# A spectral mixer beside a shift-MLP on one core: the order of the first stage, and the place of the last layer norm

## The chip, the cores and the metric

One Trainium2 chip, one of its cores. The metric is device microseconds of one execution; a kernel is run several times, and the median is taken. Engines are named as in the profile: PE is TensorE (PEld its weight loads), DVE is VectorE, ACT is ScalarE, POOL is GpSimd, SP is SyncE, which here issues the DMAs.

## The reference

x is 1 x 2048 x 448 in float32 (S = 2048 tokens, D = 448), w1 and w2 are 448 x 448, w3 is 448 x 1792, w4 is 1792 x 448, w_r and w_i are 2048 x 225.

```python
def _A_ref(x, w_r, w_i):                       # spectral branch
    X = rfft2(x, axes=(-2, -1))
    X = X * (w_r + 1j * w_i)
    return irfft2(X, s=(S, D), axes=(-2, -1))

def _B_ref(x, w1, w2, w3, w4):                 # shift-MLP branch
    h = gelu_tanh(layernorm(x) @ w1)           # 2048 x 448
    c = D // 4                                 # 112: four quarters of the columns
    g0 = h[:, :, 0*c:1*c] shifted by +1 token, zeros at the edge
    g1 = h[:, :, 1*c:2*c] shifted by -1
    g2 = h[:, :, 2*c:3*c] shifted by +2
    g3 = h[:, :, 3*c:   ] shifted by -2
    x1 = x + concatenate([g0, g1, g2, g3]) @ w2
    h2 = gelu_tanh(layernorm(x1) @ w3) @ w4
    return x1 + h2

xn = layernorm(A_x)                            # no weights, eps 1e-5
return A_x + _A_ref(xn, A_w_r, A_w_i) + _B_ref(xn, B_w1, B_w2, B_w3, B_w4)
```

## The kernel before

**Tiles.** The tokens lie in 16 blocks of 128 rows, `xb(b)`. The first stage goes over four groups of four blocks, `GRP = [[14,15,0,1],[2,3,4,5],[6,7,8,9],[10,11,12,13]]`, here called group 0 to 3 (in the prediction the first, second and third group are 0, 1 and 2). Each float32 product is made as three float16 products of high and low halves: `PASS = ((0,0),(0,1),(1,0))`, a high half being a cast copy and a low half the rest after subtracting it.

**The first stage, for one group.** `norm1` takes statistics of the four blocks (lines 309 and 310, DVE; `stats1` can take some of them earlier), forms `va` and a first approximation `vy` of the inverse root (lines 333 to 336), the negative mean `nma` (338), and normalises each block in place (line 348 on DVE or POOL, line 345 on ACT, as its list of engines says). It returns two pieces of work that POOL does later: `refine` (lines 356 to 365: small steps that refine the root and end in `gsc`, the scale for the gelu) and `scales` (lines 369 to 376). `turn_pe` transposes the group on PE, 16 transposes of 128 x 128 in four banks (line 396); `turn_copy` makes the high half on ACT (406) and the low half on DVE (407). `w1_in` makes the 44 products with w1 (line 446). `w1_unit` takes one block from there: gelu (465) and high half (466) on ACT, low half on DVE (467), and a transposing DMA on SP's queue (470) that brings the block's h into `hT`.

**The second product.** `w2_tile(b)` makes twelve products (line 486) in the order k = 2, 0, 1, 3 of the quarters, since quarter k reads h of the tokens b - SHIFT[k]; line 488 adds the result to x. Tile 0 needs h of groups 0 and, for its last quarter, block 2, which is the first of group 1; tile 1 needs for its last two quarters blocks 2 and 3. The third of the DMAs of group 1 and later ones are not needed by these two tiles.

**Weights.** `squares` and `powers` find a power-of-two scale of each weight matrix: ACT sums squares, PE adds over partitions (line 254, a product with one column), DVE makes the exponent. `split_w` then makes high and low halves, on engines chosen by its arguments: for w1 the first half on DVE, then ACT with DVE (lines 284, 285) or, for t = 2 and 3, POOL's scaling (279), ACT's copy (281) and POOL's subtraction (282); for w2 quarters 2 and 0 wholly on POOL (274 to 276), quarters 1 and 3 on POOL, ACT and POOL.

**Later stages.** `ln2` is the second layer norm of four blocks: it centres x (line 511 on the engine of its list, 509 for ACT), and makes the two halves (519 on ACT, 520 and 522 on DVE) and a transposing DMA (524). `front` (products with w3, line 417; gelu 731, halves 733 and 734) and `back` (products with w4, line 753) are the channel MLP over eight pairs of blocks G and seven pieces fp. `do_fold`, `step1_in` and `step1` (lines 543 to 579) prepare and make the first transform of the spectral branch: ACT normalises, POOL folds (554 to 557), ACT and DVE make the halves xh (564, 565), PE multiplies (574). These stand between pieces of the MLP, for G = 0 to 2. `w_scale` reads the spectral weights' largest value through a stage buffer of side 1.

**What sets the order.** A scheduler orders each engine's instructions by its own model of time. `behind(key)` restricts it: what is written inside is issued after the instructions noted in `after[key]`. It is an order of issue and not a wait at run time. The lists `PACE`, `FOLD`, `WMAX` and `LATE` give, for the folds, the spectral weights and the last `ln2`, the piece (G, fp) of the MLP behind which a step is issued. Engines work their queues in order. PSUM banks are taken by tags ("mm", "tr", "acc", "sp"), two of each.

**Ahead of all** stand matmuls on a constant, `warm_up` and `warm_rows` (lines 789 and 794), which compute nothing.

Of the kernel before, what the change touches and what calls it, by code (L numbers as in the profile page):

```python
# [36 lines left out]
LATE = [(0, 6), (0, 6), (1, 2), (1, 2)]  # L37
# [84 lines left out]
def body(tc, nc, x, wf, w1, w2, w3, w4, c_g, c_n, c_small, out):  # L122
# [145 lines left out]
    def split_w(hi, lo, src, s, low=None, high=None):  # L268
# [4 lines left out]
        if high is P:  # L273
            P.tensor_scalar(out=src, in0=src, scalar1=s, scalar2=0.0, op0=ALU.mult, op1=ALU.add)
            P.tensor_scalar(out=hi, in0=src, scalar1=1.0, scalar2=0.0, op0=ALU.mult, op1=ALU.add)
            i = P.tensor_tensor(out=lo, in0=src, in1=hi, op=ALU.subtract)
            return (i.ins,)
# [46 lines left out]
    def norm1(g, apply, seen=0, mid=None):  # L324
# [13 lines left out]
        i = V.scalar_tensor_tensor(out=nm, in0=mv[:, :n, 0], scalar=-1.0, in1=y[:, n:], op0=ALU.mult, op1=ALU.mult)  # L338
        if mid:
            mid()  # L340
# [14 lines left out]
        def refine():  # L355
# [9 lines left out]
            P.tensor_scalar(out=gsc[:, 4 * g:4 * g + 4], in0=r[:, n:], scalar1=r1, scalar2=None, op0=ALU.mult)  # L365
# [13 lines left out]
        return refine, scales  # L379
# [60 lines left out]
    def w1_in(g, units, ts, passes=range(3)):  # L440
        for p in passes:
            for t in ts:
                for i, pm in units:
                    wi, xi = ((0, 0), (0, 4), (4, 0))[p]
                    if t < 3 or p != 1:
                        T.matmul(pm[:, :D], xTs[g][:, xi + t, 128 * i:128 * i + 128], w1p[:, wi + t],  # L446
                                 start=t == 0 and p == 0, stop=t == 3 and p == 2)
# [9 lines left out]
    def w1_unit(g, i, pm=None):  # L457
# [7 lines left out]
        A.activation(out=pm, in_=pm, func=AF.Gelu_apprx_tanh, scale=gsc[:, c:c + 1])  # L465
# [8 lines left out]
    def w2_tile(b):  # L474
        pm = bank("sp", f"pw2_{b}")
        n = 0
        for k in (2, 0, 1, 3):
# [7 lines left out]
            for hi, wi in ((0, 0), (0, 1), (1, 0)):  # L485
                T.matmul(pm[:, :D], hT[g][:112, 4 * hi + k, o:o + 128], w2p[:, wi, k], start=n == 0, stop=n == 11)  # L486
                n += 1
        V.scalar_tensor_tensor(out=xb(b), in0=xb(b), scalar=cs[:, CS[b]:CS[b] + 1], in1=pm[:, :D],
                               op0=ALU.mult, op1=ALU.add)

    def ln2(bs, engines, pins=None):
# [8 lines left out]
        for m in range(0, n, 2):  # L500
            w = stage(f"y{b0 + m}", 8 * 448, (b0 + m) // 2 % 2, F16)
# [289 lines left out]
    def warm_rows(n):  # L791
        for i in range(n):
            for h, to in ((0, wps), (64, wps2)):
                T.matmul(to, wsrc[h:h + 64, 0:128], wsrc[h:h + 64], start=True, stop=True)

    wps2 = bank("mm", "wps2")
    warm_up(12)
    warm_rows(1)
    warm_up(2)
    warm_rows(2)  # L800
    warm_up(WARM - 21)
# [35 lines left out]
    with behind("p1"):  # L837
        pts = [turn_pe(0, t) for t in range(4)]
# [3 lines left out]
    for t in range(4):  # L842
        with behind("w1", t - 1):
            turn_copy(0, t, pts[t])
        with behind("a0", t):
            after["w1", t] = split_w(w1p[:, t], w1p[:, 4 + t], w1s[:, t], s1, P if t > 1 else V) if t else (hi, low())
    h1 = pc.tile([128, 1], F32, name="h1")
    V.tensor_scalar(out=h1, in0=s1, scalar1=2.0 ** -5, scalar2=None, op0=ALU.mult)
    for t in range(4):
        w1_in(0, list(enumerate(first)), [t])  # L850
    with behind("ws"):
        n1[0][0]()
    with behind("w1", 1):
# [3 lines left out]
    with behind("n", 1):  # L857
        s2, r2 = powers(m2, 1, "2", first[0][:, 448:512], lambda: stats1(2, [0]))
    with behind("np", 1):
        n1[1][0]()  # L860
        for k in (2, 0):
            after["w2p"] = split_w(w2p[:, 0, k], w2p[:, 1, k], w2s[:112, k], s2[:112], high=P)
    with behind("p2"):
        T1(1)
# [4 lines left out]
    p12, eps12 = s12[:, 1:2], s12[:, 2:3]  # L869
    with behind("a1"):  # L870
        w1_unit(0, 0, first[0])
        n1.append(norm1(2, [P, V, A, P], 1))
    with behind("a1"), behind("n", 2):
        for k in range(1, 4):
            w1_unit(0, k, first[k])
    with behind("na", 2):
        for k in (1, 3):
            split_w(w2p[:, 0, k], w2p[:, 1, k], w2s[:112, k], s2[:112], P)
# [6 lines left out]
    n1[2][0]()  # L885
    with behind("np", 2):
        n1[0][1]()
    for n in n1[1:]:
        n[1]()
# [3 lines left out]
    for k in range(4):  # L893
        w1_unit(2, k)
# [6 lines left out]
    for b in range(4):  # L901
# [130 lines left out]
```

## Time and profile before

| | us |
|---|---|
| median of 3 runs | 416.75 |
| lowest, highest | 415.66, 417.54 |
| the profiled execution | 416.13 |
| its span (all instructions) | 414.3 |
| PE busy | 407.0 |
| DVE busy | 301.2 |
| ACT busy | 245.8 |
| POOL busy | 115.9 |

The profile is of one execution; its span begins with the first and ends with the last instruction, and 1.8 us of the execution lie outside it. The times in rows are from the span's start. A row of the timeline has the start, the busy time, the engine, the line, the operation with the names of what it writes and reads, the shapes and how many instructions are put together (xN); a bracket tells the idle time of the engine before it and what ended it. "x2mem" and "hs" are both buffers of h before its transposing DMA. The mean granted PE clock of the execution was 0.999 of full speed.

### The profile page before, as it was taken

The numbers are of one execution on the slowest core, as the hardware profiler recorded it, in microseconds if no ns is written. First come the engines' busy times: TensorE is split into PE (matmuls) and PEld (weight loads), VectorE is DVE, ScalarE is ACT, GpSimd is POOL, SyncE is SP. The second block draws the span as 40 slices with busy tenths as digits, with TensorE's granted clock in tenths as the row PEclk, the third lists the DMA queues.
The fourth block names the chain that finished last, engine by engine and source line by source line (L and its number), as shares of the span: only waits on it lengthen the run. The fifth ranks groups of instructions, "written<-read, shape, count | busy, mean of one in ns | idle before, by whom it ended". The sixth has DMA issues, their size and how long they took to land.

```text
span 414.3 us, 8527 instructions
## 1 busy us (share of the span) xinstructions
PE 407.0 (98%) x3309; PEld 289.4 (70%) x3309; DVE 301.2 (73%) x636; ACT 245.8 (59%) x425; POOL 115.9 (28%) x206
## 2 busy tenths in 40 slices
PE   8999999999999999999999999999999999999996
PEld 3655555765667677776888788787777776677885
DVE  5998999798775867752688889865777687667122
ACT  4588969964649765642578888864444334342321
POOL 2797720101046647400032121210212221221000
PEclk9999999999999999999999999999999999999999
DMA  8959798804931565215056665620000213224001
GB/s 282 349 184 189 148 170 319 162 37 94 219 91 45 134 221 181 91 46 140 14 129 168 152 162 142 147 70 10 2 0 2 68 31 126 90 67 134 24 0 46
DMA packets 53496, 48.53 MB, mean 117 GB/s; under 512 B 37600, under 2 KB 48480, under 8 KB 53456
## 3 DMA queue, kind: packets, MB, share of 16 engines
q1 hardware_dynamic: 53456, 47.99, 43.0%
q8 instruction: 26, 0.43, 0.4%
q14 instruction: 14, 0.11, 0.1%
HBM read 35.52 MB, written 3.67 MB: 95 GB/s over the span
## 4 chain that ended last, share of the span: by engine, by line
PE 88%; DVE 6%; ACT 2%; DMA 2%; issue 1%; POOL 0%
PE pw L417 31%; PE acc L753 30%; PE pw L486 9%; PE pw L446 4%; PE pu L676 3%; PE ps L574 2%; PE pe L696 2%; PE pp L631 2%; PE px L648 2%; PE py L718 2%; DVE sta L309 1%; DMA xt<-x 1%; DMA h<-hs 1%; DVE xT L407 1%; ACT xf L548 1%
## 5 line engine op out<-in xcount | busy, mean ns | idle before, releaser
L417 PE MATMUL pw<-x2mem,w3p 128*128 128x256 f16 x1232 | 149.1, 273 | 0.0
L753 PE MATMUL acc<-w4p,hf 128*128 128x448 f16 (+1 forms) x714 | 138.0, 341 | 0.0
L417 PEld LDWEIGHTS <-w3p 128*128 128x128 f16 x1232 | 118.6, 98 | 18.9
L753 PEld LDWEIGHTS <-hf 128*128 128x128 f16 x714 | 69.4, 98 | 48.5 <-DVE hf L734 0.3
L731 ACT ACTIVATE pw<-pw,pe 128x512 f32<-128x512 f32 x56 | 36.8, 657 | 68.5 <-PE pw L417 68.5
L734 DVE SCALAR_TENSOR_TENSOR hf<-pw,h,hf 128x512 f16<-128x512 f32 x56 | 41.9, 748 | 42.9 <-ACT hf L733 42.5
L486 PE MATMUL pw<-w2p,h 112*128 112x448 f16 x192 | 39.8, 352 | 0.9 <-DMA h<-hs 0.9
L733 ACT ACTIVATE hf<-pw,h 128x512 f16<-128x512 f32 x56 | 38.2, 684 | 1.2
L657 POOL TENSOR_TENSOR z<-te 128x450 f32<-128x450 f32 x16 | 16.3, 1018 | 74.0 <-DVE te L655 74.0
L446 PE MATMUL pw<-w1p,xT 128*128 128x448 f16 x176 | 35.0, 352 | 0.1
L703 POOL TENSOR_TENSOR e<-e 128x226 f32<-128x226 f32 x16 | 11.3, 708 | 77.6 <-ACT e L700 74.7
L486 PEld LDWEIGHTS <-h 112*128 112x128 f16 x192 | 18.6, 98 | 17.0 <-DMA h<-hs 1.1
L446 PEld LDWEIGHTS <-xT 128*128 128x128 f16 x176 | 17.1, 98 | 16.2 <-DVE xT L407 0.4
L638 ACT ACTIVATE pf<-pp 64x450 f16<-64x450 f32 x32 | 17.3, 541 | 16.6 <-DVE pf L639 8.1
L700 ACT ACTIVATE e<-pe 128x452 f32<-128x452 f32 x16 | 8.8, 548 | 26.6 <-PE pe L696 26.5
L639 DVE TENSOR_TENSOR pf<-pp,pf 64x450 f16<-64x450 f32 x32 | 19.9, 622 | 5.3 <-ACT pf L638 5.0
L653 ACT ACTIVATE te<-px 64x450 f32<-64x450 f32 x32 | 17.2, 539 | 0.5
L557 POOL TENSOR_TENSOR f<-xr 128x452 f32<-128x452 f32 x16 | 16.9, 1078 | 0.6
L711 DVE TENSOR_TENSOR vh<-e,vh 128x448 f16<-128x448 f32 x16 | 10.0, 625 | 9.7 <-ACT vh L710 9.7
L554 POOL TENSOR_TENSOR xr<-xf 128x452 f32<-128x452 f32 x8 | 9.1, 1137 | 24.9 <-issue 24.2
L705 DVE TENSOR_TENSOR e<-e 128x113 f32<-128x113 f32 x16 | 9.5, 594 | 7.8 <-POOL e L703 7.8
L565 DVE TENSOR_TENSOR xh<-f,xh 128x452 f16<-128x452 f32 x16 | 12.8, 842 | 2.0 <-ACT xh L564 2.0
(173 smaller groups left out, 604.2 us busy)
## 6 DMA issues: line engine op xcount, KB each, us to landing
wc<-wf SPq DMA_DIRECT2D x32, 225.0 KB, 3.7
wl<-wf SPq DMA_DIRECT2D x8, 450.0 KB, 4.0
xf<-x SPq DMA_DIRECT2D x8, 448.0 KB, 4.1
xt<-x SPq DMA_DIRECT2D x3, 896.0 KB, 12.6
w3raw<-w SPq DMA_DIRECT2D x3, 896.0 KB, 15.7
xr<-x SPq DMA_DIRECT2D x12, 224.0 KB, 2.5
out<-xr SPq DMA_DIRECT2D x12, 224.0 KB, 2.0
gn<-c_g SPq DMA_DIRECT2D x16, 128.0 KB, 3.3
```

Of the source, the lines that this page charges most:

```text
L417: T.matmul(ps_out, wp[:, wi + t, cols], xT[:, xi + t, tok], start=t == 0 and wi + xi == 0, stop=t == 3 and wi == 4)
L446: T.matmul(pm[:, :D], xTs[g][:, xi + t, 128 * i:128 * i + 128], w1p[:, wi + t], start=t == 0 and p == 0, stop=t == 3 and p == 2)
L486: T.matmul(pm[:, :D], hT[g][:112, 4 * hi + k, o:o + 128], w2p[:, wi, k], start=n == 0, stop=n == 11)
L557: P.tensor_tensor(out=f[:, :, k:k + 2].rearrange("p b s d -> p s b d"), in0=u[:, :, 0], in1=u[:, :, 1], op=op)
L638: A.activation(out=hi, in_=src, func=AF.Copy)
L639: V.tensor_tensor(out=lo, in0=src, in1=hi, op=ALU.subtract)
L653: A.activation(out=e[64 * h:64 * h + 64], in_=px_[64 - 64 * h:128 - 64 * h, :2 * DF], func=AF.Copy)
L657: P.tensor_tensor(out=z, in0=t[:, 0], in1=t[:, 1], op=ALU.add)
L731: A.activation(out=pm, in_=pm, func=AF.Gelu_apprx_tanh, scale=r3)
L733: i = A.activation(out=h[:, 0], in_=pm, func=AF.Copy, scale=h3)
L734: j = V.scalar_tensor_tensor(out=h[:, 1], in0=pm, scalar=h3, in1=h[:, 0], op0=ALU.mult, op1=ALU.subtract)
L753: m = T.matmul(to, h[:, hi, o:o + 128], w4p[0][:, wi, f, r], start=f == 0 and n == 0, stop=f == 13 and n == 2)
```

## The change

It does the following.

- The warm-up is 25 full matmuls; before it was 18 full ones and three pairs of matmuls on half the rows, mixed.
- Group 0: two of the four turns are made first, then four products (t = 0, first pass), then the other two turns, then the rest. The low half of w1's second quarter (t = 1) is made by POOL, through a scaled copy in a scratch row, instead of by DVE.
- `refine` ends before `gsc`, which is a piece of its own (`gain`). POOL's `refine` of group 0 runs uncut after w1's low halves, and that of group 1 uncut after `gsc` of group 0; w2's halves come after `gsc` of group 1: first the scaling of quarters 1 and 3, then scaling and high half of 2 and 0, then the low halves.
- Group 1: two of its turns are placed before the last pass of t = 3 of group 0's products, the other two behind. `powers` of w2 has a bank of its own, and its scalar steps on DVE stand between DVE's low copies.
- Group 2: two of its statistics are taken after group 1's copies, and va, vy and nma stand ahead of the low halves of h of blocks 14 and 15. Its normalisations are on POOL once and DVE three times (before POOL, DVE, ACT, POOL); the DVE ones stand behind these two low halves.
- In group 0, each gelu from the third on is issued behind the halves of the block two before it.
- `w2_tile` 0 and 1 are made in full before group 2's products with w1 (`behind("w2", 1)`); before, the scheduler mixed them.
- The last `ln2` (blocks 12 to 15) is issued behind the MLP's pieces (2,2) to (2,5) instead of (0,6) and (1,2), in the program after the folds, with ACT centring all four blocks, and both its buffers on side 0 of the stage.

```diff
@@ -34,7 +34,7 @@
 FOLD = [(0, 5), (1, 0), (1, 1), (1, 3), (1, 4), (1, 6), (2, 0), (2, 2)]
 PIN = [("a3",), ("a3",), ("a3",), ("a3",)]
 WMAX = [(1, 4), (1, 5), (1, 6), (2, 0), (2, 1), (2, 2), (2, 3), (2, 4)]
-LATE = [(0, 6), (0, 6), (1, 2), (1, 2)]
+LATE = [(2, 2), (2, 3), (2, 4), (2, 5)]
 HS = 3
 INV, LAG = 4, 2
 EVAC, FILL = 0, 100000
@@ -272,9 +272,13 @@
             return i.ins, lambda: V.scalar_tensor_tensor(out=lo, in0=src, scalar=s, in1=hi, op0=ALU.mult, op1=ALU.subtract).ins
         if high is P:
             P.tensor_scalar(out=src, in0=src, scalar1=s, scalar2=0.0, op0=ALU.mult, op1=ALU.add)
-            P.tensor_scalar(out=hi, in0=src, scalar1=1.0, scalar2=0.0, op0=ALU.mult, op1=ALU.add)
-            i = P.tensor_tensor(out=lo, in0=src, in1=hi, op=ALU.subtract)
-            return (i.ins,)
+            i = P.tensor_scalar(out=hi, in0=src, scalar1=1.0, scalar2=0.0, op0=ALU.mult, op1=ALU.add)
+            return i.ins, lambda: P.tensor_tensor(out=lo, in0=src, in1=hi, op=ALU.subtract)
+        if isinstance(low, bass.AP):
+            P.tensor_scalar(out=low, in0=src, scalar1=s, scalar2=0.0, op0=ALU.mult, op1=ALU.add)
+            i = A.activation(out=hi, in_=src, func=AF.Copy, scale=s)
+            j = P.tensor_tensor(out=lo, in0=low, in1=hi, op=ALU.subtract)
+            return i.ins, j.ins
         if low is P:
             i = P.tensor_scalar(out=src, in0=src, scalar1=s, scalar2=0.0, op0=ALU.mult, op1=ALU.add)
             after["ws"] = (i.ins,)
@@ -336,8 +340,10 @@
         V.tensor_scalar(out=yi, in0=yi, scalar1=-1, scalar2=0x5F3759DF, op0=ALU.mult, op1=ALU.add)
         nm = pc.tile([128, n], F32, name=f"nma{b0}")
         i = V.scalar_tensor_tensor(out=nm, in0=mv[:, :n, 0], scalar=-1.0, in1=y[:, n:], op0=ALU.mult, op1=ALU.mult)
+        after["c", g] = (i.ins,)
         if mid:
-            mid()
+            with behind("c", g):
+                mid()
         for k, b in enumerate(bs):
             y_, m_ = y[:, n + k:n + k + 1], nm[:, k:k + 1]
             if apply[k] is A:
@@ -362,7 +368,10 @@
             P.tensor_tensor(out=z, in0=z, in1=q, op=ALU.mult)
             P.tensor_scalar(out=z, in0=z, scalar1=-0.5 * 0.375 ** 3, scalar2=1.5 * 0.375, op0=ALU.mult, op1=ALU.add)
             P.tensor_tensor(out=r, in0=z, in1=w, op=ALU.mult)
-            P.tensor_scalar(out=gsc[:, 4 * g:4 * g + 4], in0=r[:, n:], scalar1=r1, scalar2=None, op0=ALU.mult)
+
+        def gain():
+            i = P.tensor_scalar(out=gsc[:, 4 * g:4 * g + 4], in0=r[:, n:], scalar1=r1, scalar2=None, op0=ALU.mult)
+            after["g", g] = (i.ins,)
 
         def scales():
             c, r1st, u = cs[:, 4 * g:4 * g + 4], w[:, 0:n], w[:, n:]
@@ -376,7 +385,7 @@
             P.tensor_scalar(out=nm1, in0=nm1, scalar1=-1.0, scalar2=None, op0=ALU.mult)
             for k, b in enumerate(bs):
                 xn_scale[b], xn_bias[b] = r1st[:, k:k + 1], nm1[:, k:k + 1]
-        return refine, scales
+        return refine, gain, scales
 
     after = {}
 
@@ -443,8 +452,9 @@
                 for i, pm in units:
                     wi, xi = ((0, 0), (0, 4), (4, 0))[p]
                     if t < 3 or p != 1:
-                        T.matmul(pm[:, :D], xTs[g][:, xi + t, 128 * i:128 * i + 128], w1p[:, wi + t],
-                                 start=t == 0 and p == 0, stop=t == 3 and p == 2)
+                        m = T.matmul(pm[:, :D], xTs[g][:, xi + t, 128 * i:128 * i + 128], w1p[:, wi + t],
+                                     start=t == 0 and p == 0, stop=t == 3 and p == 2)
+        return m
 
     hs_buf = [p1.tile([128, 2, 4, 128], F16, name=f"hs{i}") for i in range(HS)]
     for t in hs_buf:
@@ -462,7 +472,8 @@
         pm = pm[:, :D]
         pv_ = pm.rearrange("p (k n) -> p k n", k=4)
         h = hs_buf[c % (HS if g == 3 else HS + 2)]
-        A.activation(out=pm, in_=pm, func=AF.Gelu_apprx_tanh, scale=gsc[:, c:c + 1])
+        with behind(0, i - 2) if g == 0 and i > 1 else contextlib.nullcontext():
+            A.activation(out=pm, in_=pm, func=AF.Gelu_apprx_tanh, scale=gsc[:, c:c + 1])
         u = A.activation(out=h[:, 0, :, 0:112], in_=pv_, func=AF.Copy, scale=h1)
         v = V.scalar_tensor_tensor(out=h[:, 1, :, 0:112], in0=pv_, scalar=h1, in1=h[:, 0, :, 0:112],
                                    op0=ALU.mult, op1=ALU.subtract)
@@ -483,8 +494,9 @@
             g, i = WHERE[src]
             o += h_at(g, i) - 1
             for hi, wi in ((0, 0), (0, 1), (1, 0)):
-                T.matmul(pm[:, :D], hT[g][:112, 4 * hi + k, o:o + 128], w2p[:, wi, k], start=n == 0, stop=n == 11)
+                m = T.matmul(pm[:, :D], hT[g][:112, 4 * hi + k, o:o + 128], w2p[:, wi, k], start=n == 0, stop=n == 11)
                 n += 1
+        after["w2", b] = (m.ins,)
         V.scalar_tensor_tensor(out=xb(b), in0=xb(b), scalar=cs[:, CS[b]:CS[b] + 1], in1=pm[:, :D],
                                op0=ALU.mult, op1=ALU.add)
 
@@ -498,7 +510,7 @@
         nm = pc.tile([128, 4], F32, tag="nm", bufs=2, name=f"nm{b0}")[:, :n]
         P.tensor_scalar(out=nm, in0=mv[:, :n, 0], scalar1=-1.0, scalar2=None, op0=ALU.mult)
         for m in range(0, n, 2):
-            w = stage(f"y{b0 + m}", 8 * 448, (b0 + m) // 2 % 2, F16)
+            w = stage(f"y{b0 + m}", 8 * 448, 0 if pins else (b0 + m) // 2 % 2, F16)
             o.append(w[:, 0:4 * D].bitcast(F32).rearrange("p (i n) -> p i n", i=2))
             y.append(w[:, 4 * D:8 * D].rearrange("p (i n) -> p i n", i=2))
             for i in range(2):
@@ -788,17 +800,7 @@
         for i in range(n):
             T.matmul(wps, wsrc[:, 0:128], wsrc, start=True, stop=True)
 
-    def warm_rows(n):
-        for i in range(n):
-            for h, to in ((0, wps), (64, wps2)):
-                T.matmul(to, wsrc[h:h + 64, 0:128], wsrc[h:h + 64], start=True, stop=True)
-
-    wps2 = bank("mm", "wps2")
-    warm_up(12)
-    warm_rows(1)
-    warm_up(2)
-    warm_rows(2)
-    warm_up(WARM - 21)
+    warm_up(WARM)
     m1, m2, m3, m4 = (pc.tile([128, n], F32, name=f"m{i}") for i, n in ((1, 4), (2, 1), (3, 4), (4, 7)))
     junk4 = row().bitcast(F16)[:, :2 * D]
     V.memset(m1, 0.0)
@@ -835,74 +837,96 @@
     with behind("n", 0):
         s1, r1 = powers(m1, 4, "1", "mm")
     with behind("p1"):
-        pts = [turn_pe(0, t) for t in range(4)]
+        pts = [turn_pe(0, t) for t in range(2)]
     h_alloc(0)
     first = [bank("mm" if k < 2 else "sp", f"pw1_0{k}") for k in range(4)]
     hi, low = split_w(w1p[:, 0], w1p[:, 4], w1s[:, 0], s1, high=V)
     for t in range(4):
+        if t == 1:
+            after["T", 0] = (w1_in(0, list(enumerate(first)), [0], [0]).ins,)
+            pts += [turn_pe(0, 2), turn_pe(0, 3)]
         with behind("w1", t - 1):
             turn_copy(0, t, pts[t])
         with behind("a0", t):
-            after["w1", t] = split_w(w1p[:, t], w1p[:, 4 + t], w1s[:, t], s1, P if t > 1 else V) if t else (hi, low())
+            after["w1", t] = split_w(w1p[:, t], w1p[:, 4 + t], w1s[:, t], s1, P if t > 1 else xr[:, 0:D]) if t else (hi, low())
     h1 = pc.tile([128, 1], F32, name="h1")
     V.tensor_scalar(out=h1, in0=s1, scalar1=2.0 ** -5, scalar2=None, op0=ALU.mult)
-    for t in range(4):
-        w1_in(0, list(enumerate(first)), [t])
+    for t in range(3):
+        w1_in(0, list(enumerate(first)), [t], range(0 if t else 1, 3))
+    after["T", 1] = (w1_in(0, list(enumerate(first)), [3], [0]).ins,)
     with behind("ws"):
         n1[0][0]()
-    with behind("w1", 1):
+    with behind("a0", 1):
         n1.append(norm1(1, [P, V, A, V]))
     with behind("w1", 3):
         squares(m2[:112], flat(w2s[:112]))
     with behind("n", 1):
-        s2, r2 = powers(m2, 1, "2", first[0][:, 448:512], lambda: stats1(2, [0]))
+        pts = [turn_pe(1, t) for t in range(2)]
+        with behind("T", 1):
+            s2, r2 = powers(m2, 1, "2", "acc", lambda: stats1(2, [0]))
+        with behind("p2"):
+            after["T", 1] = (w1_in(0, list(enumerate(first)), [3], [2]).ins,)
     with behind("np", 1):
+        n1[0][1]()
+    with behind("g", 0):
         n1[1][0]()
-        for k in (2, 0):
-            after["w2p"] = split_w(w2p[:, 0, k], w2p[:, 1, k], w2s[:112, k], s2[:112], high=P)
-    with behind("p2"):
-        T1(1)
+        n1[1][1]()
+    pts += [turn_pe(1, 2), turn_pe(1, 3)]
+    for t in range(4):
+        turn_copy(1, t, pts[t])
+    with behind("g", 1):
+        for k in (1, 3):
+            P.tensor_scalar(out=w2s[:112, k], in0=w2s[:112, k], scalar1=s2[:112], scalar2=0.0, op0=ALU.mult, op1=ALU.add)
+        lows = [split_w(w2p[:, 0, k], w2p[:, 1, k], w2s[:112, k], s2[:112], high=P) for k in (2, 0)]
+    for hi, low in lows:
+        with behind("g", 1):
+            low()
     s12 = pc.tile([128, 4], F32, name="s12")
     V.tensor_tensor(out=s12[:, 0:1], in0=h1, in1=s2, op=ALU.mult)
     V.scalar_tensor_tensor(out=s12[:, 1:2], in0=r1, scalar=2.0 ** 5, in1=r2, op0=ALU.mult, op1=ALU.mult)
     V.tensor_scalar(out=s12[:, 2:3], in0=s12[:, 0:1], scalar1=s12[:, 0:1], scalar2=EPS, op0=ALU.mult, op1=ALU.mult)
     p12, eps12 = s12[:, 1:2], s12[:, 2:3]
+    stats1(2, [1])
     with behind("a1"):
-        w1_unit(0, 0, first[0])
-        n1.append(norm1(2, [P, V, A, P], 1))
-    with behind("a1"), behind("n", 2):
-        for k in range(1, 4):
+        n1.append(norm1(2, [P, V, V, V], 2, lambda: [w1_unit(0, k, first[k]) for k in range(2)]))
+        for k in range(2, 4):
             w1_unit(0, k, first[k])
-    with behind("na", 2):
-        for k in (1, 3):
-            split_w(w2p[:, 0, k], w2p[:, 1, k], w2s[:112, k], s2[:112], P)
+    for k in (1, 3):
+        with behind(0, 3):
+            A.activation(out=w2p[:, 0, k], in_=w2s[:112, k], func=AF.Copy)
+        with behind("np", 2):
+            i = P.tensor_tensor(out=w2p[:, 1, k], in0=w2s[:112, k], in1=w2p[:, 0, k], op=ALU.subtract)
+    after["w2p"] = (i.ins,)
     h_alloc(1)
     for k in range(4):
         w1_unit(1, k)
     T1(2)
     with behind("h", 1, 3):
         load_w3([3])
-    n1[2][0]()
-    with behind("np", 2):
-        n1[0][1]()
-    for n in n1[1:]:
-        n[1]()
+    with behind("w2p"):
+        n1[0][2]()
+        n1[1][2]()
+        for f in n1[2]:
+            f()
+    for b in range(2):
+        w2_tile(b)
     with behind("a2"):
         n1 = [norm1(3, [P, P, P, P])]
     h_alloc(2)
-    for k in range(4):
-        w1_unit(2, k)
+    with behind("w2", 1):
+        for k in range(4):
+            w1_unit(2, k)
     for k in range(4):
         with behind(*(("a2",), ("a2",), (2, 0), (2, 1))[k]):
             squares(m3[:, k:k + 1], w3raw[:, k])
     s3, r3 = powers(m3, 4, "3", "mm")
     h3 = pc.tile([128, 1], F32, name="h3")
     V.tensor_scalar(out=h3, in0=s3, scalar1=2.0 ** -5, scalar2=None, op0=ALU.mult)
-    for b in range(4):
+    for b in range(2, 4):
         w2_tile(b)
     turn(3)
-    n1[0][0]()
-    n1[0][1]()
+    for f in n1[0]:
+        f()
     ln2([0, 1], [A, P])
     with behind("t", 3), behind("h", 2, 3), behind("b0"):
         for i in range(4):
@@ -956,7 +980,6 @@
     for i in range(4):
         P.memset(xh_buf[i][:, 904:], 0.0)
     mlp([1, 2], ahead=AH, tags=("mm", "tr"))
-    ln2(range(12, 16), [P, A, P, A], LATE)
     for b in range(0, NB, 2):
         do_fold(b)
         step1_in(b)
@@ -964,6 +987,7 @@
         with behind("m", *PACE[b // 2]):
             step1(b)
             step1(b + 1)
+    ln2(range(12, 16), [A] * 4, LATE)
     with behind("X", 14):
         wm = w_scale()
     close("pfd")
```

## The prediction

> **What bounds the kernel now.** I read the page's busy shares and chain first, then the table by stretches, then TensorE's waits, and only then single instructions.
>
> ```profile
> span 414.3 us, 8527 instructions
> PE   407.0 (98%) x3309; PEld 289.4 (70%) x3309; DVE 301.2 (73%) x636; ACT 245.8 (59%) x425; POOL 115.9 (28%) x206
> PE 88%; DVE 6%; ACT 2%; DMA 2%; issue 1%; POOL 0%
> 9.50:22.30 12.80, 12.56 (x80) 8.40 (x81) 11.54 (x39) 7.80 (x14) 8.78 (x24) 1.00 1.02 350
> 30.90:46.70 15.80, 14.94 (x85) 8.27 (x84) 13.78 (x39) 13.42 (x23) 10.92 (x39) 1.00 0.99 184
> 46.70:128.00 81.30, 81.30 (x542) 51.84 (x541) 69.44 (x168) 58.89 (x97) 18.19 (x37) 1.00 0.61 146
> 128.00:139.00 11.00, 9.96 (x84) 7.01 (x83) 8.82 (x10) 9.40 (x19) 10.17 (x10) 1.00 0.39 86
> 139.00:200.00 61.00, 61.00 (x531) 45.07 (x529) 37.21 (x57) 31.64 (x56) 19.86 (x20) 1.00 0.43 130
> PE ps L574 <- DVE xh L565: 1.0, 2, 0.7
> PE pw L486 <- DMA h<-hs: 0.9, 1, 0.9
> ```
>
> The first three lines are the page: TensorE (PE) is busy 407.0 us of the span. The five rows of the table after them are the stretches: length, then busy time of PE, PE's weight loads, DVE, ACT and POOL. PE fills 46.7 to 128 and 139 to 200 entirely. So no step elsewhere gains anything there, and a microsecond lost before 46.7 is not made up later. What the change can win is PE's idle time in the stretches that it rearranges: 0.24 + 0.86 + 1.04 = 2.1 us, or somewhat more, since ends of matmuls are modelled; I allow 3. The last two lines are PE's waits that make most of it: for DVE's low half of the folded rows, and for one transposing DMA. The matmuls themselves are almost the same set in both kernels, so the sum is one of idle time.
>
> **The warm-up.** Six half-height matmuls (line 794) become full ones and the order is plain.
>
> ```profile
> 1.22 5.30 PE L789 MATMUL wps<-wsrc 128*128 128x512 f16 x12 [1.22 <-DVE wsrc L186]
> 8.12 1.04 PE L789 MATMUL wps<-wsrc 128*128 128x512 f16 x4
> 9.53 0.35 PE L254 MATMUL pm<-pt,ones 128*128 128x1 f32 x2 [0.38 <-DVE pt L248]
> ```
>
> Early ones cost about 0.44 us each (5.30/12), the last four at most 0.26 (1.04/4). The speed changes near 7 us, so about 14 of the 25 are slow: 1.22 + 14 × 0.44 + 11 × 0.21 to 0.26 ends at 9.7 to 10.2; with the finer figure of 0.436 it is 9.6. The next matmul starts at 9.53 and had 0.38 us in hand, which is the cover. Cost 0 to +0.6; I take **+0.1**, since the modelled ends make 1.04/4 too long.
>
> **First group: products between turns, one low half moved to POOL.**
>
> ```profile
> 9.75 1.95 PE L396 MATMUL pta<-ident,xt 128*128 128x128 f32 x16
> 11.53 8.49 PE L446 MATMUL pw<-w1p,xT 128*128 128x448 f16 x44
> 10.42 1.08 ACT L406 ACTIVATE xT<-pta 128x512 f16<-128x512 f32 x2 [0.67 <-PE pta L396]
> 13.14 0.89 POOL L279 TENSOR_SCALAR w1s<-w1s,pe 128x448 f32<-128x448 f32 x1 [1.69 <-ACT w1p L281]
> 15.52 1.03 POOL L282 TENSOR_TENSOR w1p<-w1s,w1p 128x448 f16<-128x448 f32 x1
> ```
>
> Sixteen transposes run from 9.75 to 11.53, 0.11 each. With only eight ahead PE is done at 10.6, and the first product needs ACT's first copy, over at about 11.0: some 0.4 us idle, early. The low half on POOL adds a scaling (0.89) and a subtraction (1.03); POOL drops the refinement steps that now stand between its low halves to behind them, so its queue is longer by about 1.9 less its waits (1.69 at 13.14). What is queued behind is POOL's normalisation of the second group, which the second group's turns wait for. I put it within 0.3 us of before. Both costs end in the wait for the transposing DMAs below and are covered by it; uncovered they are +0.4 and +0.3.
>
> **Second group: VectorE's low copies are mixed with the scalar chain of w2's scale.**
>
> ```profile
> 21.57 2.60 DVE L407 TENSOR_TENSOR xT<-pta,xT 128x512 f16<-128x512 f32 x4 [0.39 <-ACT xT L406]
> 24.23 6.36 PEld L446 LDWEIGHTS <-xT 128*128 128x128 f16 x35 [0.43 <-DVE xT L407]
> 28.71 0.16 DVE L338 SCALAR_TENSOR_TENSOR nma<-mva,vy 128x4 f32<-128x4 f32 x1
> ```
>
> The four copies run back to back to 24.17 and PE resumes at 24.23. With four small scalar steps between them, at most 0.16 each if they are like the nma row, the copies end about 0.5 later, so this group's products end near 31.4. TensorE then has 21 w2 products and 16 transposes before the transfer that decides; 0.5 is again covered.
>
> **Second and third groups: VectorE's chain ahead of the low halves, w2 before the third group's products.** This is the large term.
>
> ```profile
> 24.21 1.68 DVE L309 BATCH_NORM_STATS2 sta<-xt 128x6 f32<-128x448 f32 x3
> 26.34 2.03 POOL L276 TENSOR_TENSOR w2p<-w2s,w2p 112x448 f16<-112x448 f32 x2
> 26.73 0.67 DVE L333 TENSOR_SCALAR va<-mva 128x4 f32<-128x4 f32 x1
> 27.50 0.89 DVE L335 TENSOR_SCALAR vy<-va 128x8 int32<-128x8 int32 x1
> 28.91 0.51 DVE L348 TENSOR_SCALAR xt<-xt,vy,nma 128x448 f32<-128x448 f32 x1
> 28.68 1.13 ACT L465 ACTIVATE pw<-pw,gsc 128x448 f32<-128x448 f32 x2 [1.55 <-POOL gsc L365]
> 26.68 6.00 SPq L470 DMA_TRANSPOSE h<-hs  x3
> 35.56 4.09 SPq L470 DMA_TRANSPOSE h<-hs  x3
> h<-hs SPq DMA_TRANSPOSE x8, 3.3
> 33.33 1.31 PE L486 MATMUL pw<-w2p,h 112*128 112x448 f16 x6 [0.85 <-DMA h<-hs]
> 40.65 6.22 PE L446 MATMUL pw<-w1p,xT 128*128 128x448 f16 x32
> 46.71 8.68 PE L486 MATMUL pw<-w2p,h 112*128 112x448 f16 x45
> ```
>
> Before, the third group's 44 products fill PE while the transposes land (the 32 at 40.65 stand behind the last w2 step of tile 1), and all is done at 46.71. Afterwards tiles 0 and 1 are finished first, and then all 44 products follow. Tile 1's last three need the sixth transposing DMA. A product takes (46.71 − 40.65)/32 = 0.189, so the stretch ends at that landing + 3 × 0.189 + 44 × 0.189 = landing + 8.9. Before, the sixth was issued at 35.56 and landed 3.3 later, at 38.9: with that landing alone the end is 47.75, **+1.0**, though no engine became slower. PE's work from 31.4 on (24 + 44 products, 16 transposes) gives the floor: 31.4 + 12.9 + 1.8 = 46.1.
>
> When is the sixth issued? SP spaces them 1.37 apart (4.09/3). The first needs the low half of block 0. It was issued at 26.68; now two statistics (0.56 each), their aggregation (about 0.3) and the five steps from va to nma stand ahead of it on DVE. Those five took 26.73 to 28.87 (the nma row above), 2.1 us; at 0.16 each they would take 0.8. From 24.75: 24.75 + 1.1 + 0.3 + (0.8 to 2.1) + 0.65 = 27.6 to 28.9. Five spacings on, the sixth is issued at 34.5 to 35.8: the earlier gain (ACT no longer waits 1.55 for a scale) evens the later start. Then three normalisations on DVE stand between the second and third low halves; at the 0.51 of the one at 28.91 they add 1.5, which SP's spacing nearly covers. Held up once by a POOL subtraction (1.02, half of 2.03) the third is issued about 31.9, the sixth 4.1 later at 36.0, landing 39.3, end 48.2: **+1.5**, the value I take, as the rows for va and vy show such holding up. Bounds: −0.6 (floor) and +3.5 (every normalisation held up).
>
> The row for va is the evidence: 0.67 for 4 columns where nma takes 0.16, ending as POOL's subtraction (26.34, two in 2.03) does, and vy again 0.89. [...]
>
> **The last layer norm (tokens of blocks 12 to 15) moves behind the folds and wholly to ACT.**
>
> ```profile
> 131.44 1.13 DVE L520 SCALAR_TENSOR_TENSOR y<-y,vs 128x64 f16<-128x64 f32 x1 [0.36 <-ACT y L519]
> 136.05 2.03 DVE L565 TENSOR_TENSOR xh<-f,xh 128x452 f16<-128x452 f32 x2
> 136.09 0.27 PE L417 MATMUL pw<-x2mem,w3p 128*128 128x256 f16 x1
> 136.72 0.73 PE L574 MATMUL ps<-csm,xh 128*128 128x128 f16 x10 [0.36 <-DVE xh L565]
> 138.13 0.73 PE L574 MATMUL ps<-csm,xh 128*128 128x128 f16 x10 [0.68 <-DVE xh L565]
> 138.70 1.91 PE L417 MATMUL pw<-x2mem,w3p 128*128 128x256 f16 x16
> L734 DVE SCALAR_TENSOR_TENSOR hf<-pw,h,hf 128x512 f16<-128x512 f32 x5 | 3.7, 748 | 6.4 <-ACT hf L733 6.4
> ```
>
> DVE's four layer-norm steps run from 131.44 up to 136.05, ahead of the low halves xh. Ten ps matmuls take 138.70 − 138.13 = 0.57, so the first ten end at 137.29 and PE idles 0.84 till 138.13; before 136.72 it idles 0.52 (136.09 plus 0.11). With those steps gone xh comes 4.6 earlier and both stalls go: **−1.4**, at least −1.0 by the waits. What is late next there would be POOL's folds (10.17 of 11.00 busy), the reason for the lower bound. The new place, between 165 and 190, has 6.4 us of DVE idle before five steps of line 734 (last row above), ACT is busy 31.64 of 61, and PE runs ahead; its four transposing DMAs also stand ahead of weight loads on SP's queue that no early step waits for. Cost 0, bound +2 if ACT's eight added steps hold a gelu that PE waits for.
>
> **Sum.** +0.1 + 1.5 − 1.4 = +0.2. The profiled execution took 416.13 (span 414.3, 1.8 around it), 0.6 below the median 416.75 of the runs shown; carried onto the median the forecast is 417.0.
>
> **Rivals.** *Faster: the first transfer comes on time.* If va to nma run free and the first DMA goes at 27.2, the sixth lands at 27.2 + 6.9 + 3.3 = 37.4, PE's floor decides (46.1 or, if the second group is not late, 45.6), and the change is 0.1 − 0.6 − 1.4 = −1.9, at best −2.4. ACT's 1.55 us wait going away speaks for it; two statistics and five steps more in front of the low half speak against it. *Slower: VectorE is held up by POOL's subtractions.* Place: the three normalisations ahead of the third low half; price 1.0 each, so with two more hold-ups than in my case the third DMA goes at 31.9 + 2.0 = 33.9, the sixth at 38.0, landing 41.3, end 50.2: +3.5 + 0.1 − 1.4 = +2.2, and up to +3 where the first low half is late as well. It outweighs the gain once the sixth DMA is issued after 35.8 and passes 0.5% from 37.9. *Slower: the layer norm stalls PE in its new place*, +1.5 + 0.1 − 1.4 + 2 = +2.2. *No change*: PE stays filled by what it has, and only the small terms remain; this lies within the forecast's case.
>
> **How the numbers follow.** 0.5%, 2.1 us, is about what a measurement of this kernel can tell from no change. My case (−0.6 to +1.7) has 0.48, all within. The faster rival has 0.20, 0.12 of it beyond −2.1. The held-up VectorE has 0.25, 0.20 of it beyond +2.1; the layer norm 0.07, 0.06 beyond. So 0.12 faster, 0.62 within, 0.26 slower. The range takes the faster rival's −2.0 and the slower one's +3: 414.8 to 419.8.
>
> **What would show it.** The trace of the changed kernel should show: no PE wait on xh near 136; a PE wait of 1.5 to 2.5 us for h before the last products of tile 1, ending near 39; the first transposing DMA at 27.6 to 28.9, the sixth about 36; the third group's products in one stretch of 44, ending near 48. I am wrong if that stretch ends before 47 (faster), or if a new PE wait stands after 139, or before 31 by over 1 us.

## The result, and the profile after

The changed kernel takes 418.87 us (median of 19 runs, 417.28 to 419.80), the kernel before 416.31 (19 runs). Over all runs the ratio is 1.0050, with a 95% interval of 1.0037 to 1.0063; the two medians by themselves are 2.6 us apart, a ratio of 1.0061, because the median of the changed kernel falls into the upper of two sets of runs. It is slower, on the border of 0.5%. The profiled executions differ by less: 417.28 against 416.13, spans 415.5 and 414.3. The rest lies in the clock that TensorE was granted: of the 19 runs 6 have a mean granted TensorE clock of 1.0 and lie near 417.3, 13 have 0.996 and lie near 419.0; of the runs of before measured beside the experiments 57 had 0.998 or more (median 415.8) and 9 had 0.996 (417.6). So at the same clock the change costs 1.5 us, and it has the lower clock in most runs instead of in one of seven. The profile below is of an execution at 1.0.

TensorE's waits:

```profile
PE pw L497 <- DMA h<-x2mem: 1.8, 2, 1.1
PE pta L405 <- DVE xt L354: 0.5, 1, 0.5
PE pw L455 <- ACT xT L415: 0.3, 1, 0.3
PE pw L497 <- DMA h<-hs: 0.2, 1, 0.2
PE pm L254 <- DVE pt L248: 0.2, 1, 0.2
```

The wait for xh is gone from the list; 2.0 us for h stand where 0.9 stood. The same in TensorE's timeline, w2 at line 497, w1 at line 455:

```profile
30.69 0.38 PE L405 MATMUL pta<-ident,xt 128*128 128x128 f32 x2
31.62 1.19 PE L405 MATMUL pta<-ident,xt 128*128 128x128 f32 x6 [0.55 <-DVE xt L354]
...
37.31 0.74 PE L497 MATMUL pw<-w2p,h 112*128 112x448 f16 x3 [0.70 <-DMA h<-x2mem]
39.19 1.88 PE L497 MATMUL pw<-w2p,h 112*128 112x448 f16 x9 [1.14 <-DMA h<-x2mem]
40.90 8.49 PE L455 MATMUL pw<-w1p,xT 128*128 128x448 f16 x44
49.23 8.68 PE L497 MATMUL pw<-w2p,h 112*128 112x448 f16 x45
```

The third group's products stand in one piece behind tiles 0 and 1 and end at 49.23; before they ended at 46.71. That is +2.52, with the first scale's matmul at 9.52 and 9.53. Why h is late, on VectorE, GpSimd and SP:

```profile
25.44 0.38 DVE L337 TENSOR_SCALAR va<-mva 128x4 f32<-128x4 f32 x1
26.39 0.97 DVE L340 TENSOR_SCALAR vy<-vy 128x8 int32<-128x8 int32 x1
27.39 0.95 DVE L342 SCALAR_TENSOR_TENSOR nma<-mva,vy 128x4 f32<-128x4 f32 x1
28.27 1.26 DVE L478 SCALAR_TENSOR_TENSOR hs<-pw,h,hs 128x448 f16<-128x448 f32 x2
29.45 2.53 DVE L354 TENSOR_SCALAR xt<-xt,vy,nma 128x448 f32<-128x448 f32 x3
26.29 2.03 POOL L276 TENSOR_TENSOR w2p<-w2s,w2p 112x448 f16<-112x448 f32 x2
29.14 2.17 POOL L898 TENSOR_TENSOR w2p<-w2s,w2p 112x448 f16<-112x448 f32 x2
29.02 4.86 SPq L481 DMA_TRANSPOSE h<-hs  x3
33.98 2.67 SPq L481 DMA_TRANSPOSE h<-x2mem  x2
36.74 4.13 SPq L481 DMA_TRANSPOSE h<-hs  x3
35.37 3.78 DMA h<-x2mem
```

Two steps on four or eight columns, vy and nma, take 0.97 and 0.95 us while GpSimd's two subtractions of line 276 run, and the three normalisations take 2.53 while the two of line 898 run. The last row is from the chain that ended last: the fifth DMA, issued at 35.37, landed at 39.15, and TensorE went on at 39.19 with the nine products that were left of the two tiles. Behind 46.7 the loss stays until 138, where it becomes smaller (in a row the length comes first, then the busy times of PE, its weight loads, DVE, ACT and POOL, then the granted clock; the rows of before stand in the prediction):

```profile
46.70:128.00 81.30, 81.30 (x533) 50.85 (x531) 66.22 (x166) 57.44 (x92) 15.90 (x35) 1.00 0.60 142
128.00:139.00 11.00, 11.00 (x93) 8.23 (x91) 5.12 (x6) 8.98 (x18) 8.86 (x9) 1.00 0.27 76
139.00:200.00 61.00, 61.00 (x531) 45.05 (x528) 40.57 (x59) 37.41 (x66) 21.83 (x22) 1.00 0.51 140
```

Between 128 and 139 TensorE is busy all the time (9.96 of 11.00 before), VectorE does 5.12 instead of 8.82; and no gap stands between 139 and 200, where the layer norm went. 2.52 less 1.36 is 1.16, and the profiled executions differ by 1.15.

### The profile page after: what moved, and what is told of

Same layout as the page of the kernel before. It is cut to its first block, busy times and chain, and to the rows that moved or that the text cites. A ratio compares the mean times of both kernels' runs of the same rounds, so it can differ in the third digit from the quotient of the medians.

```text
span 415.5 us, 8527 instructions
## 1 busy us (share of the span) xinstructions
PE 407.4 (98%) x3310; PEld 289.8 (70%) x3310; DVE 299.1 (72%) x637; ACT 246.9 (59%) x426; POOL 115.1 (28%) x205
## 4 chain that ended last, share of the span: by engine, by line
PE 92%; DVE 3%; DMA 2%; POOL 2%; issue 0%; ACT 0%
PE pw L426 32%; PE acc L765 31%; PE pw L497 8%; PE pw L455 6%; PE pu L688 3%; PE ps L586 3%; PE pe L708 2%; PE pp L643 2%; PE px L660 2%; PE py L730 2%; DMA xt<-x 1%; DMA h<-x2mem 1%; DVE sta L313 1%; DVE xT L416 1%; PE pta L405 1%; POOL w2p L898 1%
## 5 line engine op out<-in xcount | busy, mean ns | idle before, releaser
L497 PE MATMUL pw<-w2p,h 112*128 112x448 f16 x192 | 39.6, 352 | 2.1 <-DMA h<-x2mem 1.8
```

What stands on the lines that cost most here:

```text
L497: m = T.matmul(pm[:, :D], hT[g][:112, 4 * hi + k, o:o + 128], w2p[:, wi, k], start=n == 0, stop=n == 11)
```

## The experiments

**The warm-up alone.** As the two sets of runs differ in their mean clock, I first suspected the warm-up, whose first matmuls take longer than its last ones (0.44 and at most 0.26 us, as in the prediction).

```diff
-    warm_up(12); warm_rows(1); warm_up(2); warm_rows(2); warm_up(WARM - 21)
+    warm_up(WARM)
```

> The kernel before with the changed kernel's warm-up alone (25 full matmuls). The profiled executions of before and after differ by 1.15 us, the medians by 2.6, and the runs of after fall in two sets: granted clock 1.0 with 417.3, and 0.996 with 419.0. Theory 1 (the warm-up makes the rest): where TensorE's speed rises late, 25 full matmuls at 0.427 end at 1.22 + 25 x 0.427 = 11.9 instead of 10.2 for the 21 slots of before, so part of the runs are 1.5 us longer and the median is 417.0 to 417.8. Theory 2 (the two sets have nothing to do with the warm-up): the median stays at 416.3, within 0.3.

Measured: 415.52 (12 runs, ratio 0.9986, interval 0.9972 to 1.0000), all at 0.998 or more. And the opposite, the old warm-up in the changed kernel:

> The changed kernel with the warm-up of before (18 full matmuls and three pairs of half height). Theory 1 (the warm-up makes the rest): the set at 0.996 goes or comes down to the other, the median is 417.3 to 417.7 instead of 418.9. Theory 2: two sets as before the edit and a median of 418.9, within 0.3.

Measured: 418.90 (9 runs, ratio 1.0054, 1.0034 to 1.0073), six of nine at 0.996. My theory 1 on this point fell twice: the new warm-up costs nothing that shows, and the two clocks don't come from it. (The 415.52 is below the 416.3 that theory 2 named; the kernel before, measured beside it, had 415.91.)

**The layer norm alone.** The kernel before, with the move of the last `ln2`:

```diff
-LATE = [(0, 6), (0, 6), (1, 2), (1, 2)]
+LATE = [(2, 2), (2, 3), (2, 4), (2, 5)]
-            w = stage(f"y{b0 + m}", 8 * 448, (b0 + m) // 2 % 2, F16)
+            w = stage(f"y{b0 + m}", 8 * 448, 0 if pins else (b0 + m) // 2 % 2, F16)
-    ln2(range(12, 16), [P, A, P, A], LATE)    # ahead of the folds
+    ln2(range(12, 16), [A] * 4, LATE)         # behind them
```

> The kernel before with the last layer norm moved as in the changed kernel, and nothing else. Theory 1: both waits of TensorE for xh near 136 go (0.52 + 0.84) and none comes: 416.3 - 1.4 = 414.9. Rival: without the front's change the stall only moves (to the folds on GpSimd or to the new place), 416.3 within 0.3.

Measured: 414.41 (12 runs), 0.9965 (0.9949 to 0.9981). In its timeline the ps matmuls stand without a gap:

```profile
135.00 0.27 PE L417 MATMUL pw<-x2mem,w3p 128*128 128x256 f16 x1
135.10 0.28 PE L574 MATMUL ps<-csm,xh 128*128 128x128 f16 x2
135.22 0.38 PE L417 MATMUL pw<-x2mem,w3p 128*128 128x256 f16 x2
135.44 1.39 PE L574 MATMUL ps<-csm,xh 128*128 128x128 f16 x22
```

So this part of the change is a gain of 1.5 us by itself, and needs nothing of the rest.

**GpSimd's subtractions moved.** In the changed kernel, the four subtractions of w2's low halves are put behind GpSimd's normalisation of group 2 and the `scales` of groups 0 and 1, so that none of the four runs while VectorE makes va to nma and its normalisations.

```diff
-    for hi, low in lows:
-        with behind("g", 1):
-            low()
...
+    with behind("np", 2):
+        n1[0][2]()
+        n1[1][2]()
+    for hi, low in lows:
+        with behind("sc", 0), behind("sc", 1):
+            low()
     for k in (1, 3):
...
-        with behind("np", 2):
+        with behind("sc", 0), behind("sc", 1):
             i = P.tensor_tensor(out=w2p[:, 1, k], in0=w2s[:112, k], in1=w2p[:, 0, k], op=ALU.subtract)
```

> The changed kernel with one thing moved on GpSimd: the four subtractions for w2's low halves stand behind its normalisation of the third group and the small steps of the scales of groups 0 and 1, so that none of them runs while VectorE makes va to nma and its three normalisations. Theory 1 (VectorE is held up by GpSimd's subtractions, and this makes the transposing DMAs late): the five steps va to nma take 0.8 to 1.2 us instead of 2.9, the three normalisations about 1.4 instead of 2.5, the first transposing DMA goes at about 27.4 instead of 29.0, the sixth at 34.3 to 35 instead of 36.7, and the third group's products end at 47.0 to 47.6 instead of 49.2: 1.6 to 2.2 us less than the changed kernel, 416.7 to 417.3. Rival (the DMAs' own spacing or the w2 halves decide): the sixth DMA still lands near 40, or the w2 products now wait for the low halves of w2, and the time stays at 418.9 within 0.5.

Measured: 415.23 (12 runs), 0.9978 (0.9963 to 0.9993) of the kernel before, so 3.6 below the changed kernel. The rows of VectorE and SP:

```profile
27.28 0.17 DVE L340 TENSOR_SCALAR vy<-vy 128x8 int32<-128x8 int32 x1
27.49 0.16 DVE L342 SCALAR_TENSOR_TENSOR nma<-mva,vy 128x4 f32<-128x4 f32 x1
28.75 1.35 DVE L354 TENSOR_SCALAR xt<-xt,vy,nma 128x448 f32<-128x448 f32 x3
31.26 2.03 POOL L276 TENSOR_TENSOR w2p<-w2s,w2p 112x448 f16<-112x448 f32 x2
32.40 0.68 DVE L479 SCALAR_TENSOR_TENSOR hs<-pw,h,hs 128x448 f16<-128x448 f32 x1 [0.52 <-ACT hs L478]
28.33 4.09 SPq L482 DMA_TRANSPOSE h<-hs  x3
10.42 0.38 PE L254 MATMUL pm<-pt,ones 128*128 128x1 f32 x2 [1.16 <-DVE pt L248]
47.77 8.68 PE L498 MATMUL pw<-w2p,h 112*128 112x448 f16 x45
```

This execution began its scales 0.9 later (10.42 against 9.52: the wait ahead of it, behind the first load of x, was 1.16 here, 0.17 in the profile after and 1.80 in that of the layer norm alone), so times are counted from the start of that matmul, the mark. The same instructions on the same operands take 0.17, 0.16 and 1.35 instead of 0.97, 0.95 and 2.53; the first DMA goes 17.91 instead of 19.50 after the mark, and the front ends 37.35 instead of 39.71 after it. Theory 1 held here: 2.36 us at the front, and 2.1 us between the runs at full clock (417.3 and 415.2). The median fell by more, as only one of 12 runs has the lower clock.

**The third group's products mixed with w2 again**, in the changed kernel:

```diff
-    for b in range(2):
-        w2_tile(b)
...
-    with behind("w2", 1):
-        for k in range(4):
-            w1_unit(2, k)
+    for k in range(4):
+        w1_unit(2, k)
...
-    for b in range(2, 4):
+    for b in range(4):
         w2_tile(b)
```

> The changed kernel with one thing undone: the third group's products are again left to the scheduler's mixing with the w2 products of tiles 0 and 1, instead of standing behind them. The transposing DMAs stay as late as in the changed kernel (first about 29.0, fifth about 35.4, landing near 39.1). Theory 1 (of the 2.5 us at the front about half is the late DMAs' effect on tiles that nothing fills, so 0.9 + 1.3 us of TensorE's idle time between 36 and 39 is filled by products whose operands are there): the third group's products end 1 to 1.8 us earlier than 49.2, and the runs at granted clock 0.996 (13 of 19 for the changed kernel) go, since these two gaps are what lets the clock fall: median 415.8 to 416.5. Rival (the operands of the third group are late too, since its normalisations are held up): the end stays at 48.8 to 49.3 and the median above 417.

Measured: 416.20 (12 runs), 1.0018 (0.9998 to 1.0037), three of 12 at 0.996; they became rarer, but the expectation that they would go did not hold.

```profile
39.23 1.31 PE L497 MATMUL pw<-w2p,h 112*128 112x448 f16 x6 [0.38 <-DMA h<-x2mem]
48.13 8.68 PE L497 MATMUL pw<-w2p,h 112*128 112x448 f16 x45
```

The products end at 48.13, 1.1 earlier, with the DMAs as late as in the changed kernel (the first at 29.08). So of the 2.5 us 1.1 are the price of tiles 0 and 1 standing ahead unfilled, and the rest remains as long as the DMAs are late. Both edits together:

> The changed kernel with both edits: GpSimd's four subtractions behind its normalisation and the scales, and the third group's products mixed with the w2 products. If the two add, TensorE's last wait for h (1.2 us in the kernel with the first edit alone) is filled as well: 415.2 - 1.0 = 414.2, at or below the kernel before with the moved layer norm alone (414.4). Rival (the sixth transposing DMA decides either way): 415.2 within 0.3.

Measured: 414.81 (12 runs), 0.9967 (0.9954 to 0.9981): 0.4 better than with the first alone, not 1.0. At the front the two do add: it ends 35.91 after the mark (45.70 less 9.79), 1.4 earlier than with the first alone. But TensorE then waited further down, for VectorE's adding of tiles 2 and 3 to x:

```profile
50.70 2.43 PE L498 MATMUL pw<-w2p,h 112*128 112x448 f16 x12 [0.28 <-DVE xt L501]
53.73 1.86 PE L498 MATMUL pw<-w2p,h 112*128 112x448 f16 x9 [0.61 <-DVE xt L501]
```

(The next expectation gives these two waits as 0.45 and 0.77; the rows have 0.28 and 0.61.) An edit that puts these two additions ahead of the second layer norm's halves and statistics:

> The changed kernel with the subtractions late and the products mixed, and with VectorE's adding of tiles 2 and 3 to x put ahead of the first layer norm's halves and of the second one's statistics (TensorE waited 0.45 and 0.77 us near 50 and 53 for these two). Theory 1 (the gain at the front was eaten by these two waits): 414.8 - 1.0 = 413.8. Rival (VectorE is full in this stretch and the waits only move): 414.8 within 0.3.

Measured: 414.03 (6 runs), 0.9950 (0.9931 to 0.9970). That is 0.8 of the 1.0 expected; the interval overlaps that of the run before it, so the size of this gain is not sure. TensorE's waits for the additions fell from 0.9 to 0.2 us in all, and a new one of 0.6 for VectorE came further down.

**Where the clock falls.** The changed kernel once more:

> The changed kernel again, one look, to see where the granted clock falls in an execution of mean clock 0.996, if this is one: theory 1 has it right behind the gaps, between 37 and 42, for about 3.4 us at half (1.6 us / 0.5); the rival has it elsewhere, or at the start.

When this was written, no trace had shown the half or the 3.4 us (1.6 / 0.5 is 3.2), nor that such gaps let the clock fall, as the expectation for the mixed products has it. It was an execution of 0.996 (418.60). Its stretches, the third number from the end being the granted clock:

```profile
36.00:37.00 1.00, 0.37 (x2) 0.00 (x0) 1.00 (x3) 1.00 (x3) 0.81 (x5) 1.00 0.98 183
37.00:38.00 1.00, 0.74 (x3) 0.21 (x3) 0.97 (x3) 1.00 (x2) 0.84 (x6) 1.00 1.19 165
38.00:39.00 1.00, 0.15 (x1) 0.11 (x2) 0.97 (x3) 0.97 (x3) 0.29 (x1) 1.00 1.13 227
39.00:40.00 1.00, 1.00 (x5) 0.45 (x4) 1.00 (x4) 1.00 (x1) 0.00 (x0) 0.78 0.99 192
40.00:41.00 1.00, 1.00 (x4) 0.45 (x3) 1.00 (x3) 0.78 (x2) 0.00 (x0) 0.50 0.97 185
41.00:42.00 1.00, 1.00 (x4) 0.41 (x3) 0.57 (x4) 0.00 (x0) 0.00 (x0) 0.50 0.88 163
42.00:43.00 1.00, 1.00 (x5) 0.35 (x3) 1.00 (x4) 0.00 (x0) 0.00 (x0) 0.51 0.98 186
43.00:44.00 1.00, 1.00 (x7) 0.54 (x6) 1.00 (x8) 0.00 (x0) 0.00 (x0) 1.00 1.02 287
```

From about 39.6 to 43.0 the clock is at half, 3.4 us, right behind three microseconds in which TensorE was busy for 1.26. That costs (0.22 + 0.50 + 0.50 + 0.49) = 1.7 us, the distance between the two sets of runs. The profile after has the same gaps (TensorE busy for 1.35 of the three microseconds) and no fall, so the gaps alone don't settle whether a run is hit. To see whether the gaps are the cause I filled them with matmuls that do no useful work, into the unused columns of tile 0's bank:

```diff
+            if b == 0 and k in (1, 3):
+                with behind("T", 2) if k == 1 else behind("k1"):
+                    for _ in range(10 if k == 1 else 16):
+                        T.matmul(pm[:, D:512], w2p[:112, 0, 2, 0:128], w2p[:112, 0, 2, 0:64], start=False, stop=False)
```

> The changed kernel with 26 small matmuls of 64 columns (into the unused last columns of tile 0's bank) in the two gaps of TensorE between 36 and 39, 10 ahead of tile 0's third quarter and 16 ahead of its fourth. They do no useful work, and the products stay where they were but for three that move behind them (0.57 us). Theory 1 (two gaps so near to each other let the granted clock fall to half for a window, in two thirds of the runs): no run or few at 0.996, all near 417.3 to 417.9. Rival (the clock of a run has nothing to do with these gaps): 0.996 in over half of the runs, and the median at 418.9 to 419.5.

Measured: 419.51 (6 runs), four of six at 0.996. As a test of the cause this one told nothing: the 26 matmuls took 1.1 us together, and the waits behind them were still 1.25 and 0.73. But its profiled execution is one of 0.996 too, and the clock fell at the same place:

```profile
35.00:40.00 5.00, 3.03 (x39) 2.08 (x38) 4.60 (x9) 4.79 (x8) 2.90 (x15) 0.90 1.06 189
40.00:45.00 5.00, 5.00 (x21) 2.32 (x20) 3.40 (x10) 1.10 (x2) 0.00 (x0) 0.76 0.99 206
```

At half clock that is (0.10 + 0.24) x 5 / 0.5 = 3.4 us again. With 36 and 34 matmuls:

> The fill of the earlier run again with enough of it: its 26 small matmuls took 0.04 us each and left 1.25 and 0.73 us of idle time between 35.7 and 39.3, so they did not fill the gaps, and 4 of 6 runs were at clock 0.996. Now 36 ahead of tile 0's third quarter and 34 ahead of its fourth (1.5 and 1.4 us; no useful work). Theory 1 (the two gaps let the granted clock fall for a window): no or few runs at 0.996, all near 418.0 (the median of the earlier fill's undisturbed runs). Rival (the clock has nothing to do with the gaps): over half of the runs at 0.996, median above 419.2.

Measured: 419.10 (6 runs), 1.0079 (1.0054 to 1.0104), one of six at 0.996. Between 35 and 40 TensorE is busy 4.12 us instead of 3.06 in the profile after:

```profile
35.00:40.00 5.00, 4.12 (x84) 3.50 (x83) 4.51 (x8) 4.71 (x9) 3.11 (x16) 1.00 1.36 173
```

The gaps are shorter, not gone: waits of 0.51, 0.36 and 0.52 for h are left up to 42. The kernel is no faster, as the fill and three products moved behind it cost 1.7 us; but the lower clock shows in one run of six, against 14 of 20 of the changed kernel. Six runs are few. With the place of the fall in two traces, I take these gaps as the cause in the changed kernel and call it likely, not shown beyond doubt. They can't be the only cause of a lower clock: the kernel before with the layer norm alone has it in four of 12 runs, with waits for h of 0.31 and 0.15 in its profile, and the last kernel below in two of seven, with none. Those profiles are of executions at full clock, so where the clock fell in these runs stays open.

**The better version.** The kernel before, with the layer norm moved and GpSimd's two subtractions of line 276 behind its two normalisations of group 2 (`behind("np", 2)`). The expectation speaks of four; the other two already stand behind these normalisations in the kernel before (from 31.96 on), and the edit moves two:

> The kernel before with the moved layer norm, and with GpSimd's four subtractions for w2's low halves behind its two normalisations of the third group. Theory 1 (VectorE's va and vy are held up by these subtractions in the kernel before too, 0.67 and 0.89 us): va to nma take about 1.2 us instead of 2.1, the second transposing DMA goes about 1 us earlier than 29.6 to 30.1, TensorE's waits of 0.3 and 0.3 us near 32 and 35 go, and the median is 0.3 to 0.7 below 414.4: 413.7 to 414.1. Rival (TensorE's waits then are for w2's low halves, which now come later): 414.4 or more.

Measured: 413.77 (7 runs), 0.9948 (0.9926 to 0.9970), better than both kernels. Against the layer norm alone (414.41; 414.2 at full clock) it is 0.4 to 0.6 better, with intervals that overlap. VectorE's chain there:

```profile
26.94 0.17 DVE L332 TENSOR_SCALAR va<-mva 128x4 f32<-128x4 f32 x1
27.21 0.23 DVE L334 TENSOR_SCALAR vy<-va 128x8 int32<-128x8 int32 x1
```

0.17 and 0.23 instead of 0.67 and 0.89 before; and TensorE has no wait for h left.

## Why the prediction was right or wrong

It forecast 417.0, within 0.5%; measured were 418.87 and 1.0050. The time lies within the range and both mechanisms were there, but one term was too small and one was missing. The sum said +0.2 us and the medians moved by 2.6. That the time still lies inside the range is luck, and not the sum's merit: the range reached to 419.8 only for the sake of the slower rival (VectorE held up by GpSimd's subtractions), and it is this rival's mechanism that came, at about half its extra price.

- **Warm-up, +0.1.** About 0: the 25 matmuls ended before the next operand came (a wait of 0.17 was left), and neither exchange made the time longer.
- **First group.** The early idle time came (0.27 by the waits, 0.4 forecast) and was covered, as said: its products and the second group's ended at 30.69, against 30.86 before. GpSimd's normalisation was not late.
- **Second group, +0.5 later.** Wrong, at no cost: the two turns placed earlier let VectorE start its copies at 20.82 instead of 21.57, which made up for the steps between them (they end at 24.00, before at 24.17).
- **The front, +1.5.** This step failed by its size: +2.5. I let one of the three normalisations be held up; two were (0.97 and 1.22, against 0.51 before), which together cost 1.2 us, near the 1.0 that I had put for one. The larger miss lies ahead of them: the five steps from va to nma took 2.9 us where I bounded them by 0.8 to 2.1 from the trace of before: both subtractions of line 276 fell on them, and before only parts of these had. So the first DMA went at 29.02 (27.6 to 28.9 forecast) and the sixth at 36.74 (36.0). The landing that decided was the fifth's (3.78 us instead of 3.3), with nine products behind it; the sixth's was covered by them. The end of 48.2 became 49.23, halfway to my slower rival's 50.2. nma, whose 0.16 had been my measure of a free step, took 0.95 (0.16 again with the subtractions moved); that it could be held up too I had left out, and it put the chain itself at risk. Why VectorE's steps are held up by GpSimd's subtractions, no run here shows.
- **What the profile of before didn't tell.** Its own front was on the long side: a wait of 0.85 for h, where the two kernels made from it by other edits waited 0.30 and 0.31 at the same place. Against these the change loses about 3.2 at the front (39.7 after the mark against 36.5), and less the 1.4 gained that is 1.8, near the 1.5 that runs at equal clock show.
- **The layer norm, −1.4.** Right: 1.36 in the profile, 1.5 alone. The rival of a stall in the new place did not come.
- **Missing: the clock.** I priced idle time by its length. In the execution of 418.60 the clock was halved for 3.4 us behind two gaps of 0.65 and 1.08, another 1.7 us, and two of three runs have the lower mean clock; that the gaps caused it is likely, not shown. This carries the result from 0.4% (1.5 us, runs at full clock) to 0.5% over all runs, and to 2.6 us in the medians.

## What to carry to other kernels

When steps on one engine become many times as long as their size asks (0.97 us instead of 0.17 here), look at which instruction of the other engine ends with them; moving that instruction in its own queue was worth 2.4 us at the front here, with the slow steps left in their order. Before putting work with late inputs ahead of work with early inputs, find the transfer that lands last and count what is left to do until then. Price the parts of a change one by one on the chip: here one part gained 1.5 us and the others lost it twice over.

## What the runs showed of the hardware

- In the profile after, two-input subtractions on GpSimd of 1.04 us held up VectorE's steps, on operands of four and eight columns, until they ended (0.95 and 0.97, against 0.16 and 0.17 with the subtractions moved). VectorE's low halves of h, with one operand in PSUM, were not held up: with the subtractions moved, the one at 32.40 begins while the second subtraction at line 276 runs (32.3 to 33.3) and keeps its 0.68. It goes the other way too: in that run GpSimd's steps on 128 x 4 took 0.42 to 0.47 beside VectorE's three normalisations, and 0.20 ahead of them.
- In the execution of 418.60 the granted clock fell to 0.50 for 3.4 us after gaps of TensorE of 0.65 and 1.08 us by its waits, with 0.74 us of work between them. In the three microseconds from 36 to 39 TensorE was busy for 1.26. The profile after, at clock 1.0, has gaps of 0.70 and 1.14 and 1.35 busy in the same stretch, and no fall. No run here isolates what decides between the two.
